# Order by hand to the last jump, a later token pass, and the last rows behind the jump, in attention with experts on one core

## The chip, the cores and the metric

The program runs on one core of a Trainium2 chip. A core has a matrix engine (TensorE, PE in the profile), a vector engine (VectorE, DVE), a scalar engine (ScalarE, ACT), GpSimd (POOL) and SyncE (SP), which only issues transfers. Each has an instruction queue of its own and works through it in order; they meet in semaphores. 16 DMA engines, shared by all queues, move data between HBM and the core's memory. The metric is the device time in microseconds (us); smaller is better.

## The reference

Block-sparse attention, then a layer of experts, in float32:

```python
# attention: 4 batches, 8 heads, 768 positions, 64 per head, blocks of 32
scores = scale * np.matmul(q, k.transpose(0, 1, 3, 2))
scores = np.where(mask, scores, -1e9)          # window, first and last block, 3 random blocks per row
attn = softmax(scores); x = attn @ v           # -> (3072 tokens, 512)
# experts: 8 of them, each token goes to its best one
expert_idx = np.argmax(x @ w_gate, axis=1)
gate_w = probs[arange(N), expert_idx]          # softmax of the logits
y = relu(x @ w1[e]) @ w2[e]                    # for the tokens of expert e: 512 -> 1024 -> 512
out = gate_w[:, None] * y
```

Which tokens go to which expert is known only at run time.

## The kernel before, in words

**Attention** takes the first 370 us or so. It is not touched, but for that its last part overlaps with the start of the experts.

**Tiles of the experts.** The tokens are sorted by expert into tiles of up to 128, of which every token has the same expert. `NS` = 21 tiles are always computed. The first `KA` = 5 are made of the tokens of the first three batches. What does not fill a tile goes to two *units* (up to 192 tokens, next to tiles 10 and 13, `AT`) and three *small tiles* (up to 32 tokens, next to tiles 10, 13 and 17, `AT_S`). Each tile, unit and small tile needs its own expert's weights, 2 MB for w1 and 2 MB for w2.

**One tile** i: `gather(i)` (L729, GpSimd) brings the token rows by an indirect transfer; `turn_x(i)` (L778) transposes them, on VectorE in blocks of 32 for later tiles; `layer1(i)` (L797, 64 matmul records, PSUM tile `hp` in two halves, then a relu into `hT` at L804); `layer2(i)` (L811, 16 records, PSUM tile `zp`; `weigh` at L816 multiplies with the gate weight into `zo`, and `put` at L826 scatters the rows by an indirect transfer on GpSimd). A small tile has `layer1_s` (`hps`, L865), `turn_h` (a transpose on PE, `tps_`, L874, slipped between the two halves of the next tile's layer 1) and `layer2_s` (`zps`, L882). A unit has `gather_u`, `turn_u` (24 transposes on VectorE, L904) and `layers_u`, which stand with a tile's layer 2 in a three-way jump on the unit's width.

**Weights.** SP issues all weight loads, in the order of the program: L758 for w1, L761 for w2. w1 and w2 have two buffers each, used in turns in the order of `orders`, which holds tiles, units and small tiles. So the load of position p + 2 waits until PE is done with position p: `fetch_after(what, layer)` asks for it behind the work that frees the buffer.

**The loop** `for i in range(NS)` puts, for each i: the gather of tile i + 3; a small tile's first layer; layer 1 of tile i + 1 with, between its halves, the transposes of tile i + 2; the small tile's second layer; gathers and transposes for coming units and small tiles; and layer 2 of tile i. At i = 2 follow two pieces that concern the rare cases and the small tiles. `judge()` (L383 to L392) counts on PE (`okp`, L386) whether all sums lie in a good range and writes `bad` and `arm` on VectorE, by which the last jump chooses between nothing more to do, some more tiles, and all of the work again in a safer way. `tokens_s()` (L704 to L711) spreads the small tiles' token numbers with a matmul (`tps`, L704) whose PSUM buffer is the one of `okp` (tag `xr`, one buffer), and makes from it the indices `gS` and `sS`.

**What sets the order.** Under `by_hand`, a manual schedule for GpSimd, PE and VectorE, the instructions of these three engines stand as the code puts them. It is closed at i = `KA` + 1 = 6. From there on a scheduler decides by its own costs, and so it may put later work ahead: for example `turn_u`, which the code has at i = 8, stands on VectorE right behind the work of `judge`, ahead of `bad`. Behind the loop is the last jump (L1064), and behind that the program's end.

Of the kernel before, what the change touches and what calls it, by code (L numbers as in the profile page):

```python
# [7 lines left out]
F32 = mybir.dt.float32  # L8
# [9 lines left out]
def kernel(  # L18
# [11 lines left out]
    nc = tc.nc  # L30
    P = 128
# [7 lines left out]
    N, DM = out.shape  # L39
# [332 lines left out]
    def judge():  # L372


        okp = ps_x.tile([1, 1], F32, name="okp", tag="xr")
        shape, total = [[4 * B * NPR, CW], [P, NT * E]], 0
        flats = (sums[:], lgn.rearrange("p t e -> p (t e)"))
        for j, (lo, hi) in enumerate(((2.0**-4, 2.0**40), (-(2.0**100), 2.0**100))):
            p, n = shape[j]
            total += p * n  # L380
            ok = mpool.tile([p, n], F32, name=f"ok{j}")
            okn = mpool.tile([p, 1], F32, name=f"okn{j}")
            nc.vector.tensor_single_scalar(ok[:], flats[j], lo, op=ALU.is_ge)  # L383
            nc.vector.scalar_tensor_tensor(ok[:], in0=flats[j], scalar=hi, in1=ok[:], op0=ALU.is_le, op1=ALU.mult)
            nc.vector.reduce_sum(okn[:], ok[:], axis=AX)
            nc.tensor.matmul(okp[:], lhsT=okn[:], rhs=ones[:p, :1], start=(j == 0), stop=(j == 1))  # L386
        bad = mpool.tile([1, 1], F32, name="bad")
        nc.vector.tensor_scalar(bad[:], okp[:], scalar1=float(total), scalar2=float(REDO), op0=ALU.not_equal, op1=ALU.mult)

        nc.vector.tensor_scalar_min(rt["more"][:], rt["more"][:], float(NC - NS))  # L390
        arm = rt["arm"] = mpool.tile([1, 1], I32, name="arm")
        nc.vector.tensor_max(arm[:], rt["more"][:], bad[:])  # L392
# [308 lines left out]
    def tokens_s():  # L701

        tp = ps_x.tile([P, KS], F32, name="tps", tag="xr")
        nc.tensor.matmul(tp[:], lhsT=rt["fourfold"][:], rhs=rt["tv"][:, NTB + 2 * KU :], start=True, stop=True)  # L704
        tv = sm.tile([P, KS], F32, name="tvS")
        nc.vector.tensor_copy(tv[:], tp[:])
        nc.vector.tensor_scalar(kept("gS", [P, KS])[:], tv[:], scalar1=0.0, scalar2=float(N - 1), op0=ALU.max, op1=ALU.min)
        none = sm.tile([P, KS], F32, name="noneS")
        nc.vector.tensor_scalar(none[:], tv[:], scalar1=0.0, scalar2=float(8 * N), op0=ALU.is_lt, op1=ALU.mult)
        nc.vector.scalar_tensor_tensor(tv[:], in0=tv[:], scalar=4.0, in1=none[:], op0=ALU.mult, op1=ALU.add)  # L710
        nc.vector.tensor_scalar(kept("sS", [P, KS])[:], tv[:], scalar1=rt["quarter"][:], scalar2=None, op0=ALU.add)  # L711
# [106 lines left out]
    def layer2(i, group):  # L818
        zp = upper["ps_z"].tile([P, DM], F32, name="zp")
        layer2_pe(i, zp)  # L820
        zo = xp.tile([P, DM], F32, name="zo")
        weigh(i, zo, zp)
        put(of("s", i, P), zo[:], group)
# [64 lines left out]
    def leave_s(k_, group):  # L888
        put(rt["sS"][:, k_ : k_ + 1], zo_s, group, out_s)
# [103 lines left out]
    for i in range(NS):  # L993
        if i == 0:
            ranks("B", TA, NT)
        gather(i + 3)
        here = AT_S.index(i) if i in AT_S else None
        if here is not None:
            layer1_s(here)
            fetch_after(("small", here), 1)  # L1000
        if i + 1 < NS:
            layer1(i + 1, lambda: turn_x(i + 2), *([turn_h] if here is not None else []))
            if i + 3 <= NS:
                fetch_after(i + 1, 1)
        if here is not None:
            layer2_s(here)
            fetch_after(("small", here), 2)
            leave_s(here, "rows_out")
        if i == 0:
            count("B")  # L1010
            layout_b()
        if i + 3 in AT:
            gather_u(AT.index(i + 3))
        if i + 3 in AT_S:
            gather_s(AT_S.index(i + 3))
        if i + 2 in AT:
            turn_u()
        if i + 2 in AT_S:
            turn_s()
        if i in AT:  # L1020

            continue
        if i + 1 in AT:


            u = AT.index(i + 1)
            zps = [upper["ps_z"].tile([P, DM], F32, name="zp") for _ in range(2)]
            zos = [xp.tile([P, DM], F32, name="zo") for _ in range(2)]
            banks = [upper["ps_h"].tile([P, DM], F32, name="hpu", tag="hp") for _ in range(2)]
            banks += [upper["ps_m"].tile([P, DM], F32, name="tpu", tag="tpg") for _ in range(2)] + zps[1:]  # L1030
            layer2_pe(i, zps[0])
            fetch_after(i, 2)
            for more in tc.Switch(index[u], 3):
                weigh(i, zos[0], zps[0])
                layers_u(u, P + more * QR // 2, banks)
                layer2_pe(i + 1, banks[1])
                weigh(i + 1, zos[1], banks[1])
            fetch_after(("unit", u), 1)
            fetch_after(("unit", u), 2)
            fetch_after(i + 1, 2)  # L1040
            put(of("s", i, P), zos[0][:], "rows_out")
            leave_u(u, "rows_out")
            put(of("s", i + 1, P), zos[1][:], "rows_out")
            continue
        layer2(i, "rows_out")
        if i + 2 <= NS:
            fetch_after(i, 2)
        if i == 1:
            tokens("B", NT, NB_)
        if i == 2:  # L1050
            judge()
            tokens_s()
        if i == 3:
            for u in range(KU):
                at = rt["xeU"][0:1, KU + u : KU + u + 1]
                index[u] = {
                    mybir.EngineType.PE: nc.tensor.value_load(at, min_val=0, max_val=2),
                    mybir.EngineType.Activation: nc.scalar.value_load(at, min_val=0, max_val=2),
                }
        if i == KA + 1:  # L1060
            by_hand.close()
    lent.close()

    for arm in tc.Switch(nc.values_load(rt["arm"][0:1, 0:1], min_val=0, max_val=REDO), REDO + 1):  # L1064
        inside = ExitStack()
        if arm < REDO:
            lend(inside, ps_h=2, ps_m=2, ps_z=2)
            last = NS + arm
            if arm > 1:
                for layer in (1, 2):  # L1070
                    fetch(NS + 1, layer)
            for i in range(NS, last):
                if i + 3 < last:
                    gather(i + 3)
                layer1(i, *([lambda: turn_x(i + 1)] if i + 1 < last else []))
                if i + 2 < last:
                    fetch_after(i, 1)
                layer2(i, "rows_out")
                if i + 2 < last:
                    fetch_after(i, 2)  # L1080
        else:
            lend(inside, ps_s=2, ps_t=1)
            attention_again()
            lend(inside, ps_h=2, ps_m=2, ps_z=2)
            ranks("A", 0, TA)
            count("A")
            layout_a()
            slots_a()
            for part in range(2):
                one_hots("A", rt["slA"], TA, KA, part)  # L1090
            tokens("A", TA, KA)
            ranks("B", TA, NT)
            count("B")
            layout_b()
            tokens("B", NT, NB_)
            tokens_s()
            for i in range(NC):
                gather(i)
                fetch(i, 1)
                fetch(i, 2)  # L1100
                turn_x(i)
                layer1(i)
                layer2(i, "rows_again")
            for j in range(KU):
                gather_u(j)
                for layer in (1, 2):
                    fetch(("unit", j), layer)
                turn_u()
                layers_u(j, MW, [upper["ps_h"].tile([P, DM], F32, name="hpu", tag="hp") for _ in range(2)] + [upper["ps_m"].tile([P, DM], F32, name="tpu", tag="tpg") for _ in range(2)] + [upper["ps_z"].tile([P, DM], F32, name="zpu", tag="zp")])
                leave_u(j, "rows_again")  # L1110
            for j in range(KS):
                gather_s(j)
                for layer in (1, 2):
                    fetch(("small", j), layer)
                turn_s()
                layer1_s(j)
                turn_h()
                layer2_s(j)
                leave_s(j, "rows_again")
        inside.close()  # L1120


# [28 lines left out]
```

## Time and profile before

| | us |
|---|---|
| time, median of 3 (lowest to highest) | 737.55 (736.49 to 738.51) |
| profiled run, span of the core | 735.2 |
| mean granted PE clock | 0.989 |
| PE busy | 708.9 |
| attention, layer 1 and layer 2 of the tiles on PE: s L233, hp L797, zp L811 | 159.5, 156.7, 134.0 |
| weight loads, 2 MB each | 54 |
| end of the last matmul, in the span | 720.05 |

A row of the profile's groups names line, engine, operation, and the tiles it writes and reads, then its count, its busy time, the mean of one in ns, and the idle time just ahead of it with what ended that. A row of the waits reads: which engine's line waited for which engine's line, us in all, times, longest. In a timeline, start and length come first; square brackets hold the idle time before, and its cause. In a table of stretches the busy times of the engines follow in the order PE, weight load, VectorE, ScalarE, GpSimd, then the granted clock, the DMA engines' share and GB/s. The digits of the slices are tenths.

### The profile page before, as it was taken

What the parts mean: (1) busy time and instruction counts of PE and PEld (TensorE: products, weight loads), DVE (VectorE), ACT (ScalarE), POOL (GpSimd) and SP (SyncE); (2) the same over time, 40 slices, a digit from 0 to 9 for tenths busy, and PEclk for the clock granted to TensorE, in tenths of its full rate; (3) what the DMA queues carried; (4) which work ended last, traced back from release to release, by engine and by line L of the source; (5) the groups of instructions that cost most, each with busy time, mean ns of one, the idle gap of its engine ahead of it and who ended that gap; (6) DMA issues with size and microseconds to landing.
All of it is one profiled execution on the core that took longest, in us unless ns stands there. A gap on an engine that the chain in (4) does not pass through costs nothing.

```text
span 735.2 us, 13091 instructions
## 1 busy us (share of the span) xinstructions
PE 708.9 (96%) x5142; PEld 455.2 (62%) x5142; DVE 398.8 (54%) x833; ACT 281.3 (38%) x454; POOL 72.4 (10%) x116
## 2 busy tenths in 40 slices
PE   7999999999999999999999899999999999999991
PEld 4555555555555555555777676776967786866750
DVE  4587778778678778999567434323124502332300
ACT  3667666766766675675411110111121121111110
POOL 6000000000000000000212111211132012111120
PEclk9999999999999999999999999999999999999996
DMA  8313323322332331292389879999779989999973
GB/s 195 76 34 86 87 65 90 86 60 50 87 88 66 87 87 48 63 396 64 83 296 330 326 267 356 309 347 348 268 286 401 376 306 363 371 395 368 391 278 112
DMA packets 117838, 154.33 MB, mean 210 GB/s; under 512 B 56307, under 2 KB 72755, under 8 KB 117748
## 3 DMA queue, kind: packets, MB, share of 16 engines
q1 hardware_dynamic: 111104, 138.23, 56.4%
q0 software_dynamic: 4512, 14.55, 5.2%
q8 instruction: 50, 0.82, 0.5%
q10 hardware_dynamic: 2132, 0.41, 0.3%
q14 instruction: 40, 0.33, 0.2%
HBM read 140.39 MB, written 12.88 MB: 208 GB/s over the span
## 4 chain that ended last, share of the span: by engine, by line
PE 81%; issue 12%; DVE 2%; POOL 2%; DMA 1%; ACT 0%; POOLq 0%
PE s L233 17%; PE op L254 17%; PE hp L797 14%; PE zp L811 10%; PE s L236 4%; PE sp L267 3%; PE xr L287 3%; PE tp L216 2%; PE hpu L811 2%; PE hpu L915 1%; PE hpu L923 1%; PE tpu L923 1%; PE tpu L915 1%; DMA ea<-x_rows,gB 1%; DVE ea L904 1%
## 5 line engine op out<-in xcount | busy, mean ns | idle before, releaser
L233 PE MATMUL s<-qT,kT 64*128 64x384 f32 x768 | 159.5, 494 | 0.9 <-ACT qT L218 0.9
L797 PEld LDWEIGHTS hp<-xgT,w 128*128 128x128 f32 x1344 | 154.7, 194 | 8.8 <-issue 6.8
L797 PE MATMUL hp<-xgT,w 128*128 128x128 f32 x1344 | 156.7, 277 | 0.9 <-ACT hT L804 0.9
L238 ACT ACTIVATE ea<-s 128x768 f32<-128x768 f32 x192 | 152.4, 812 | 7.3 <-PE s L236 5.5
L778 DVE STREAM_TRANSPOSE xgT<-xg 32x128 f32<-32x128 f32 x256 | 77.5, 303 | 128.9 <-PE hp L797 62.1
L811 PE MATMUL zp<-w,hT 128*128 128x512 f32 x304 | 134.0, 593 | 0.7 <-DMA w<-in_moe_w_dram 0.7
L244 DVE TENSOR_TENSOR esum<-esum,ea 128x768 f32<-128x768 f32 x128 | 122.6, 958 | 14.7 <-ACT ea L238 1.3
L254 PE MATMUL op<-ea,v_sb 128*64 128x384 f32 x768 | 129.3, 486 | 0.0
L254 PEld LDWEIGHTS op<-ea,v_sb 128*64 128x64 f32 x768 | 55.1, 137 | 68.8 <-issue 68.8
L811 PEld LDWEIGHTS zp<-w,hT 128*128 128x128 f32 x304 | 56.3, 190 | 65.5 <-issue 65.3
L233 PEld LDWEIGHTS s<-qT,kT 64*128 64x128 f32 x768 | 67.2, 190 | 38.4 <-issue 33.6
L274 DVE RECIPROCAL r<-ss 128x128 f32<-128x128 f32 x96 | 82.2, 912 | 1.3 <-ACT ss L269 1.3
L804 ACT ACTIVATE hT<-hp 128x512 f32<-128x512 f32 x40 | 23.9, 597 | 127.7 <-PE hp L797 115.8
L244 DVE TENSOR_TENSOR esum<-ea 128x768 f32<-128x768 f32 x32 | 30.6, 957 | 63.1 <-ACT ea L238 63.1
L236 PE MATMUL s<-pen,oh 64*128 64x384 bf16 x384 | 63.2, 326 | 0.0
L816 ACT ACTIVATE zo<-zp,xg 128x512 f32<-128x512 f32 x19 | 13.1, 687 | 125.4 <-PE zp L811 118.3
L259 ACT COPY oT<-op 128x384 f32<-128x384 f32 x32 | 15.3, 479 | 106.3 <-PE op L254 106.3
L236 PEld LDWEIGHTS <-oh 64*128 64x128 bf16 x384 | 18.9, 95 | 26.0 <-issue 1.2
L904 DVE STREAM_TRANSPOSE ea<-ea 32x128 f32<-32x128 f32 x48 | 13.8, 296 | 35.9 <-DMA ea<-x_rows,gB 35.3
L826 POOL DMA_INDIRECT out_dram<-zo,sB x16 | 16.1, 1008 | 171.3 <-ACT zo L816 136.4
L287 PEld LDWEIGHTS xr<-mix,oT 128*64 128x64 f32 (+1 forms) x372 | 24.0, 139 | 10.7 <-issue 10.7
L729 POOL DMA_INDIRECT xg<-x_rows,gA x5 | 6.1, 1226 | 220.6 <-ACT ea L238 219.4
(275 smaller groups left out, 450.9 us busy)
## 6 DMA issues: line engine op xcount, KB each, us to landing
w<-in_moe_w_dram SPq DMA_DIRECT2D x54, 2048.0 KB
k_sb<-in_k_dram SPq DMA_DIRECT2D x32, 192.0 KB
v_sb<-in_v_dram SPq DMA_DIRECT2D x16, 384.0 KB
x_rows<-xb SPq DMA_DIRECT2D x16, 384.0 KB
q_sb<-in_q_dram SPq DMA_DIRECT2D x30, 192.0 KB
sums<-ss SPq DMA_DIRECT2D x32, 3.0 KB
q_sb<-in_q_dram ACTq DMA_DIRECT2D x2, 192.0 KB
xg<-x_rows,gB POOLq DMA_INDIRECT x19, 7.7
```

Source lines behind the costliest of these rows:

```text
L233: nc.tensor.matmul(s[:, hh, :CW], lhsT=kT[r, c * P : (c + 1) * P], rhs=qT[r, cols], start=True, stop=False)
L236: nc.tensor.matmul(s[:, hh, :CW], lhsT=oh[r, c, :], rhs=pen[r, cols], start=False, stop=True)
L238: nc.scalar.activation(e, s[:, :, :CW], AF.Exp, scale=scale)
L244: nc.vector.tensor_add(t[:], es[(n, half, 0)] if c == 1 else t[:], e)
L254: nc.tensor.matmul(op[hh * D : (hh + 1) * D, :], lhsT=v_sb[:, hh, c, :], rhs=e[:, hh, :], start=(c == 0), stop=(c == NCH - 1),)
L267: nc.tensor.matmul(sp[hh * D : (hh + 1) * D, :], lhsT=ones[:], rhs=esum[:, hh, :], start=True, stop=True)
L274: nc.vector.reciprocal(r[:, m * P : (m + 1) * P], ss[:, m * P : (m + 1) * P])
L287: nc.tensor.matmul(xr[j * M_ : (j + 1) * M_, m, :], lhsT=oT[:, m * P + j * M_ : m * P + (j + 1) * M_], rhs=mix[:, pr, :], start=True, stop ...
L778: nc.vector.transpose(xT[d, :, t], xg[t, :DM].rearrange("p (c q) -> p c q", c=DB)[:, :, d])
L797: nc.tensor.matmul(hp[:, m, :], lhsT=st[i]["w1"][:, c, fb * P : (fb + 1) * P], rhs=st[i]["xT"][:, c, :], start=(c == 0), stop=(c == DB - 1),)
L804: nc.scalar.activation(hT[:, g * (FB // 2) : (g + 1) * (FB // 2), :], hp[:], AF.Relu)
L811: nc.tensor.matmul(zp[:], lhsT=st[i]["hT"][:, fb, :], rhs=st[i]["w2"][:, fb, :], start=(fb == 0), stop=(fb == FB - 1),)
```

## The change

Three edits. First, the hand order holds for the whole loop, up to the last jump. Second, the small tiles' token pass comes two tiles later, at i = 4, away from `judge`; `judge` stays at i = 2. Third, the last tile's result goes into a part of the unit's result buffer (`zo_u`), and its rows are put out behind the last jump, so that the jump does not come after that transfer in the order of GpSimd. In the rare case that does all of the work again, the indices are set to values outside the output, so that this late transfer writes nothing.

```diff
-        layer2(i, "rows_out")
+        if i + 1 < NS:
+            layer2(i, "rows_out")
+        else:
+
+            zp = upper["ps_z"].tile([P, DM], F32, name="zp")
+            layer2_pe(i, zp)
+            weigh(i, zo_u[:, 0, :], zp)
         if i + 2 <= NS:
             fetch_after(i, 2)
         if i == 1:
             tokens("B", NT, NB_)
         if i == 2:
             judge()
+        if i == 4:
             tokens_s()
...
-        if i == KA + 1:
-            by_hand.close()
+    by_hand.close()
     lent.close()
 
     for arm in tc.Switch(nc.values_load(rt["arm"][0:1, 0:1], min_val=0, max_val=REDO), REDO + 1):
...
                 leave_s(j, "rows_again")
+
+            nc.vector.memset(rt["sB"][:], 2 * N)
         inside.close()
+    put(of("s", NS - 1, P), zo_u[:, 0, :], "rows_out")
```

In the code's order, small tile 0 is followed by layer 1 of tile 12 and then layer 2 of tile 11 (i = 11), since tile 10 has its layer 2 inside the unit's jump and the loop goes on to the next i. The same holds for small tile 1 with tiles 15 and 14.

## The prediction

> **What bounds the kernel now.** I read the page first: is one engine full, and where is it not?
>
> ```profile
> PE 708.9 (96%) x5142; PEld 455.2 (62%) x5142; DVE 398.8 (54%) x833; ACT 281.3 (38%) x454; POOL 72.4 (10%) x116
> ...
> PE   7999999999999999999999899999999999999991
> ...
> PEclk9999999999999999999999999999999999999996
> DMA  8313323322332331292389879999779989999973
> ```
>
> TensorE (PE) is 96% busy, so time can come or go only where it stands still or its clock falls. The DMA row says more: from slice 22 on (the expert layers) the 16 DMA engines are nearly full too. A change of order there can turn a transfer in time into one that PE waits for. Next, all waits of PE:
>
> ```profile
> PE tps L704 <- DVE bad L388: 3.1, 1, 3.1
> ...
> PE tps__6201 L874 <- ACT ea L869: 0.9, 1, 0.9
> PE hp L797 <- ACT hT L804: 0.9, 2, 0.5
> PE zp L811 <- DMA w<-in_moe_w_dram: 0.7, 1, 0.7
> PE zps L882 <- ACT ea L875: 0.5, 1, 0.5
> ```
>
> This is what a better order can win in the expert layers: about 6 us, half of it in the token pass. Its stretch in the timeline:
>
> ```profile
> 411.36 0.30 PE L386 MATMUL okp<-ones,okn 64*1 64x1 f32 x4
> 414.76 0.38 PE L704 MATMUL tps<-tvB,fourfold 128*128 128x3 f32 x2 [3.10 <-DVE bad L388]
> 415.01 5.45 PE L797 MATMUL hp<-xgT,w 128*128 128x128 f32 x32
> ```
>
> The token matmul shares a PSUM buffer with `okp`, so it waits until VectorE has read `okp` into `bad`; VectorE was in the unit's 24 transposes (L904) until 414.5. The 32 matmuls behind it take 5.45 us, where the same 32 take 3.84 elsewhere: the granted clock fell to 0.5 for 3.41 us. So this place costs 3.1 + 1.6 = 4.7 us.
>
> Last, the stretch behind the first small tile, where the order will differ, PE and then the weight loads:
>
> ```profile
> 544.08 1.93 PE L865 MATMUL hps<-w,ea 128*32 128x256 f32 x32
> 545.94 3.84 PE L797 MATMUL hp<-xgT,w 128*128 128x128 f32 x32
> ...
> 554.24 1.96 PE L882 MATMUL zps<-w,ea 128*32 128x128 f32 x64
> 556.12 7.13 PE L811 MATMUL zp<-w,hT 128*128 128x512 f32 x16
> ```
>
> ```profile
> 544.18 0.37 SPq L761 DMA_DIRECT2D w<-in_moe_w_dram  x1
> 546.58 8.13 SPq L758 DMA_DIRECT2D w<-in_moe_w_dram  x2
> ```
>
> The loads at 544.18 and 546.58 are w2 of tile 11 and w1 of tile 12 (the group of two also holds w1 of 13, issued 554.34). Their landing events in the trace: w2 of the small tile 548.12, w2 of 11 555.88, w1 of 12 561.03, w1 of 13 566.88. A 2 MB w1 alone lands 8.1 us after issue; here it took 14.45, as it lands 5.1 us after the load ahead of it. A small tile needs 4 MB of weights like any other but gives PE only 1.95 + 1.9 us of work, so the loads fall behind there.
>
> **What the Trainium skill says.** "DMA: Bandwidth & Descriptors", "Queues, rings and completion order": each DMA engine takes a ring's descriptors in ring order. The landings above, in order of issue and 5 to 7 us apart, agree; so an early need of PE does not make a late load come sooner. "TensorE: Matmul & The Clock Gate", "HAM oscillation": an idle gap of about 3.4 us halves the clock[...]. The trace shows 3.10 us of idling, 3.41 us at 0.5 and 1.6 us lost: it agrees, with a slightly shorter gap. "Runtime: NRT & Kernel Launch", "Instruction fetch mechanics": a taken branch to code that isn't held must fetch it; at the last jump GpSimd stands 2.7 us behind its branch. "Perfetto Trace Analysis", "DMA Instruction — SWDGE (GPSIMD)": an indirect transfer's row ends with its descriptors, not with its data; the last put is 1.00 us long and lands 3.99 us after its start.
>
> **Part 1: the token pass two tiles later.** `tokens_s` now runs after layer 2 of tile 4, when `bad` is long written, and nobody needs its result before the first small gather, over 40 us on. The 3.1 us wait goes, and the cold clock with it: -4.7. The bad/arm operations also come ahead of the 24 transposes. These wait for later gathers now, but still lie 10 us or more ahead of the unit's first matmul, beside tiles that keep PE busy: 0.
>
> **Part 2: the hand order up to the end.** Comparing the instruction lists of both kernels engine by engine, the order of SP's weight loads is the same in both. PE's changes at three places.
>
> (a) Third small tile. Its transpose slips between the halves of layer 1 of tile 18, as in the first two. The waits of 0.95 and 0.46 go, a 0.47 wait like the one at the first two comes; the 0.72 us before the last `zp` goes, since its w2 is asked for sooner against its use. -2.1 + 0.5 = -1.7 (rounded up from -1.66).
>
> (b) First and second small tile. Before: `zps`, layer 2 of 11, layer 1 of 12 and 13. After: `zps`, layer 1 of 12, layer 2 of 11, layer 1 of 13. So PE wants w1 of 12 at the end of `zps`, 556.2, instead of at 563.1. It lands at 561.0: a new wait of 4.8 us, where the old order had 2.1 to spare. Can the load come sooner? It is issued when `hps` frees its buffer, just as before, behind the same two loads. If the queue were spaced as loads elsewhere (5.15 per w1, 6.3 per w2, 10.4 from issue when alone) it would be there 3.5 us after `zps`. One unit gather (two transfers at 541 to 542) moves out of this stretch, which helps a little: I take 4.3, range 3.5 to 4.9. For the second small tile the trace has the end of `zps` at 622.1 and w1 of 15 landed at 626.06: 4.0, by the even spacing 3.5; I take 3.9. Behind the waiting matmul stand layer 2 of 11 (or 14), whose weights are there, and everything after it. PE's queue is in order, so nothing of this is hidden; nor is it won back, as PE was solid to the end.
>
> (c) Third small tile again: layer 2 of 18 now comes before, not in the middle of, layer 1 of 20, 4 us sooner. Its w2 landed at 692.54 in the trace with PE there at 695.20, and the buffer that it loads into is freed by the same `zps`: 0 to 2 us of wait, I take 1.2. The second half of layer 1 of 18, or its first, may wait some tenths for its w1 (0 to 1): 0.2.
>
> Sum of new waits: 4.3 + 3.9 + 1.2 + 0.2 = +9.6.
>
> (d) Clock. If 3.1 us of idling sufficed once, about 4 should twice. Each costs at most the 1.6 measured; less when the half-speed stretch begins in the idle time. Range 0 to 3.2, I take 2.9.
>
> **Part 3: the last rows behind the jump.** Let T be the end of the last `zp`, 720.05 before. Before: ScalarE's weighing to T+0.8, put at T+1.05, landing T+5.0; GpSimd's end-of-loop wait for all its transfers ends there; 1.4 us semaphore work, the branch, 2.7 us fetch, a drain of 4.97 us from 729.43 to 734.40, end at T+15.2. After: that wait ends when put and gather of the tile before have landed, T+2.7 (722.79 in the trace), so 2.3 us sooner. Then the same 1.4 and 2.7, then the put, 0.7 + 1.0 us, and the drain. The put's landing, 3.99 from its start at about T+7.6, lies beside the drain. -2.3 + 1.7 = -0.6. If GpSimd's wait still covers something as late as the old put: +1.7; if the weighing's semaphore costs more, +2; if the branch work all lies beside the last matmul: -4.
>
> **Sum.** -4.7 - 1.7 + 9.6 + 2.9 - 0.6 = +5.5: 737.55 + 5.5 = 743.0 us.
>
> **Rivals.** *Clock holds.* The waits come, but the clock stays up: 743.0 - 2.9 = 740.1; with the waits at their low ends (7.0 in place of 9.6) 737.5. For: the gate looks at windows that run freely. Against: the 3.1 us gap did trip it.
>
> *Loads in time (the faster side).* No new wait: 737.55 - 4.7 - 1.7 - 0.6 = 730.5. For: alone such a load takes 8.1 us, and w1 of 12 is issued 9.6 us before PE wants it. Against: the queue ahead of it is unchanged, the DMA row shows nines there, and the busy share from 557 to 584 us is full:
>
> ```profile
> 557.00:584.00 27.00, 27.00 (x159) 19.80 (x157) 13.52 (x45) 3.08 (x5) 3.89 (x4) 1.00 1.01 384
> ```
>
> *More waits.* Waits at their upper ends (4.9 + 4.2 + 2 + 1 = 12.1), clock 3.2 and a tail of +2: -4.7 - 1.7 + 12.1 + 3.2 + 2 = +10.9, 748.4. For: each wait of PE delays the free of a buffer and with it later loads. Against: those loads have 5 to 12 us in hand.
>
> **How the numbers follow.** Forecast 0.60, clock holds 0.20, loads in time 0.12, more waits 0.08. The bounds of 0.3% are 735.3 and 739.8. Faster: the third case and a little of the second's low end with a cheap tail, 0.14. Same: the second case below 739.8 and the low end of the first, 0.17. Slower: 0.69. The range from 736.5 to 747.5 leaves out the loads in time and most of the last case: under 2 in 10.
>
> **What would show it.** In the changed profile: no wait at L704, and the 32 matmuls behind the judge back at 3.84; the chain and PE's waits headed by L797 waiting for `w<-in_moe_w_dram`, twice about 4 us, right after each of the first two `zps`, followed by `hp` groups longer than their 3.84 per 32; from T to the end about 14.5 us. No such waits at L797 would overthrow (b), and with it the sign. A wait at `zp` L811 of more than 2 us would mean that I mis-sized (c).

## The result, and the profile after

The changed kernel takes 746.91 us (median of 4, 744.98 to 748.07) against 737.08 us (median of 4) for the kernel before: the ratio is 1.0128, with a 95% interval of 1.0099 to 1.0156. It is slower by 9.8 us; the forecast was 5.5. A later set of runs gave 745.17 against 736.16, ratio 1.0134 (1.0104 to 1.0163).

The page first, slices and engines:

```profile
PE 710.3 (96%) x5142; PEld 456.8 (61%) x5142; DVE 397.7 (54%) x833; ACT 281.2 (38%) x454; POOL 72.0 (10%) x116
...
PE   7999999999999999999999999999979997999891
PEld 4555555555555555555876677677767767766560
...
PEclk9999999999999999999999999999999999999997
DMA  8313333331233232391499999999599979999963
```

In the PE row, the two sevens in slices 30 and 34 are new. They stand where the first two small tiles are. In these two slices the DMA row is at nine; in the slice just ahead of each it is at five and at seven. Now all waits of PE (line waited, line waited for, sum, times, longest):

```profile
PE hp L797 <- DMA w<-in_moe_w_dram: 9.0, 3, 4.4
...
PE zp L811 <- DMA w<-in_moe_w_dram: 2.5, 1, 2.5
...
PE hp L797 <- ACT hT L804: 0.9, 2, 0.5
```

The waits at L704, L874 and L882 are gone, as they should be; in their place PE waits for weights, 11.5 us in all. PE's timeline at the judge, then at the first, second and third small tile:

```profile
411.21 0.31 PE L386 MATMUL okp<-ones,okn 64*1 64x1 f32 x4
411.44 3.84 PE L797 MATMUL hp<-xgT,w 128*128 128x128 f32 x32
```

```profile
549.40 1.96 PE L882 MATMUL zps<-w,ea 128*32 128x128 f32 x64
555.10 9.01 PE L797 MATMUL hp<-xgT,w 128*128 128x128 f32 x64 [3.75 <-DMA w<-in_moe_w_dram]
```

```profile
610.33 2.52 PE L865 MATMUL hps<-w,ea 128*32 128x256 f32 x32
...
621.07 1.95 PE L882 MATMUL zps<-w,ea 128*32 128x128 f32 x64
627.40 8.71 PE L797 MATMUL hp<-xgT,w 128*128 128x128 f32 x64 [4.38 <-DMA w<-in_moe_w_dram]
```

```profile
673.74 3.81 PE L797 MATMUL hp<-xgT,w 128*128 128x128 f32 x32 [0.87 <-DMA w<-in_moe_w_dram]
...
690.13 7.31 PE L797 MATMUL hp<-xgT,w 128*128 128x128 f32 x64
699.90 7.13 PE L811 MATMUL zp<-w,hT 128*128 128x512 f32 x16 [2.46 <-DMA w<-in_moe_w_dram]
```

Behind the judge there is no wait left and the 32 matmuls take 3.84 us. Behind each of the first two `zps` PE stands still about 4 us, and the 64 matmuls then take 9.01 and 8.71 us; the same 64 take 7.31 us at 690.13. By the landing events w2 of 11 is there at 549.85 and w1 of 12 at 554.96, 5.1 us behind it: PE starts layer 1 of 12 at 555.10. Layer 2 of 11, whose weights were there long before, stands behind it in PE's order and starts at 563.95. The table of stretches shows the clock there (PEclk is the number ahead of the DMA share), with one stretch behind the third small tile to compare:

```profile
549.00:566.00 17.00, 13.25 (x138) 11.79 (x137) 8.92 (x33) 2.16 (x4) 4.84 (x5) 0.90 1.03 402
610.00:640.00 30.00, 25.16 (x237) 20.67 (x237) 8.35 (x28) 4.09 (x8) 4.93 (x5) 0.94 1.01 377
664.00:708.00 44.00, 40.67 (x287) 27.44 (x286) 14.53 (x48) 6.06 (x11) 5.00 (x5) 1.00 1.00 379
```

Clock 0.90 over 17 us is 3.4 us at half speed; 0.94 over 30 us is 3.6. The sum, by the two profiles (from the start of `okp` to the last `zp`, then the tail):

| step | forecast | in the profile |
|---|---|---|
| token pass: wait and half-speed stretch gone | -4.7 | -4.8 |
| third small tile and last `zp`: waits gone | -1.7 | -2.1 |
| new waits for weights: tile 12, 15, 18 layer 1, 18 layer 2 | 4.3 + 3.9 + 0.2 + 1.2 = 9.6 | 3.75 + 4.38 + 0.87 + 2.46 = 11.5 |
| half-speed stretches | 2.9 | 1.7 + 1.4 = 3.1 |
| second small tile's first layer, 2.52 for 2.27 | none | 0.3 |
| last `zp` to the end | -0.6 | 15.3 for 15.15: 0.1 |
| sum | 5.5 | 8.1 (spans 743.2 and 735.2: 8.0) |

The profiled run was the quickest of its four; the median adds 1.9 us (0.8 us in the later set) that no profile of this kernel shows.

### The profile page after: what moved, and what is told of

The parts are those of the page before. It is cut to its first block, busy times and chain, and to the rows that moved or that the text cites. A ratio compares the mean times of both kernels' runs of the same rounds, so it can differ in the third digit from the quotient of the medians.

```text
span 743.2 us, 13102 instructions
## 1 busy us (share of the span) xinstructions
PE 710.3 (96%) x5142; PEld 456.8 (61%) x5142; DVE 397.7 (54%) x833; ACT 281.2 (38%) x454; POOL 72.0 (10%) x116
## 4 chain that ended last, share of the span: by engine, by line
PE 80%; issue 12%; DMA 3%; POOL 1%; DVE 1%; ACT 0%; POOLq 0%
PE s L233 17%; PE op L254 17%; PE hp L797 14%; PE zp L811 11%; PE s L236 4%; PE sp L267 3%; PE xr L287 3%; PE tp L216 2%; PE hpu L811 2%; DMA w<-in_moe_w_dram 2%; DMA out_dram<-zo,sB 1%; PE tpu L923 1%; PE hpu L923 1%; PE hpu L915 1%; PE tpu L915 1%
## 5 line engine op out<-in xcount | busy, mean ns | idle before, releaser
L797 PE MATMUL hp<-xgT,w 128*128 128x128 f32 x1344 | 158.7, 279 | 9.9 <-DMA w<-in_moe_w_dram 9.0
L259 ACT COPY oT<-op 128x384 f32<-128x384 f32 x32 | 15.3, 478 | 106.0 <-PE op L254 106.0
L267 PE MATMUL sp<-esum,ones 128*64 128x384 f32 x128 | 27.7, 512 | 0.0
L287 PE MATMUL xr<-mix,oT 128*64 128x136 f32 (+1 forms) x372 | 27.7, 279 | 0.0
```

Source lines behind the costliest of these rows:

```text
L267: nc.tensor.matmul(sp[hh * D : (hh + 1) * D, :], lhsT=ones[:], rhs=esum[:, hh, :], start=True, stop=True)
L287: nc.tensor.matmul(xr[j * M_ : (j + 1) * M_, m, :], lhsT=oT[:, m * P + j * M_ : m * P + (j + 1) * M_], rhs=mix[:, pr, :], start=True, stop ...
L797: nc.tensor.matmul(hp[:, m, :], lhsT=st[i]["w1"][:, c, fb * P : (fb + 1) * P], rhs=st[i]["xT"][:, c, :], start=(c == 0), stop=(c == DB - 1),)
```

## The experiments

**Only the token pass** (built on the kernel before):

```diff
         if i == 2:
             judge()
+        if i == 4:
             tokens_s()
```

> Only the token pass is moved, from tile 2 to tile 4; order by hand still ends at tile 6, and the last put stands before the jump. My step (part 1): the 3.1 us wait at L704 goes and with it the half-speed stretch, 4.7 us in all, so about 732.5 us (ratio about 0.994). Rival: the time comes back later as waits for weights, since the loads are issued when PE frees their buffers and the DMA engines are nearly full: then 735 to 737.

Measured: 733.17 us against 736.44, ratio 0.9962 (0.9949 to 0.9975), so 1.8 to 3.8 us less. The direction is that of part 1, the size is smaller than 4.7. The timeline shows both:

```profile
410.39 0.30 PE L386 MATMUL okp<-ones,okn 64*1 64x1 f32 x4
410.63 3.84 PE L797 MATMUL hp<-xgT,w 128*128 128x128 f32 x32
```

```profile
PE hp L797 <- issue: 1.4, 1, 1.4
...
PE tps__6201 L874 <- ACT ea L869: 0.5, 1, 0.5
...
PE zp L811 <- DMA w<-in_moe_w_dram: 0.3, 1, 0.3
```

The wait and the slow matmuls are gone in full, and they did not turn into waits for weights (0.3 us, 0.7 before), which was the rival. One standstill of 1.4 us at a layer 1 is new, with no releaser in the profile. From `okp` to the last put this profile is 4.05 us shorter (410.39 to 716.08, against 411.36 to 721.10), which is the 4.7 and 0.8 of smaller waits less that standstill. What the standstill is was not settled, nor why the times differ by less still.

**Only the order by hand up to the jump:**

```diff
-        if i == KA + 1:
-            by_hand.close()
+    by_hand.close()
```

> Only the order by hand reaches to the last jump; token pass at tile 2 and last put as before. Theory: this edit alone carries the whole loss. Layer 1 of tile 12 (15) comes ahead of layer 2 of 11 (14) and waits about 4 us for its w1 each time, with a half-speed stretch behind each. The wait at L704 goes in this kernel too, since the unit's transposes no longer stand ahead of bad on VectorE; some tenths of a wait for bad stay. So 746 to 748 us, as the changed kernel. Rival 1: without moving the token pass the 3.1 us and the cold clock stay, so 751 to 752. Rival 2: the loss is in the late put: then about 737 or faster.

Measured: 745.99 us against 736.44, ratio 1.0153 (1.0132 to 1.0174): this edit alone carries the whole loss.

```profile
PE hp L797 <- DMA w<-in_moe_w_dram: 10.5, 3, 4.8
...
PE zp L811 <- DMA w<-in_moe_w_dram: 2.1, 1, 2.1
...
PE tps L704 <- DVE more_f L390: 0.2, 1, 0.2
```

The last line is of interest: with the token pass still right behind the judge, the wait at L704 is 0.2 us, not 3.1. The 24 transposes no longer stand ahead of `bad`. So in the changed kernel the later token pass brings some tenths at most; the hand order alone had already removed that wait. Rival 1 (the 3.1 us stay) falls, and so does rival 2 (the loss is in the late put). The waits behind the first two small tiles are longer here than in the changed kernel's profile:

```profile
555.68 9.57 PE L797 MATMUL hp<-xgT,w 128*128 128x128 f32 x64 [4.81 <-DMA w<-in_moe_w_dram]
...
628.25 9.01 PE L797 MATMUL hp<-xgT,w 128*128 128x128 f32 x64 [4.67 <-DMA w<-in_moe_w_dram]
```

By the clock records of the trace, the half-speed stretch at the first of them is 6.83 us long; at the second, and at both places in the changed kernel, it is 3.41 us.

**Only the last put behind the jump:**

```diff
-        layer2(i, "rows_out")
+        if i + 1 < NS:
+            layer2(i, "rows_out")
+        else:
...
+            weigh(i, zo_u[:, 0, :], zp)
...
+    put(of("s", NS - 1, P), zo_u[:, 0, :], "rows_out")
```

> Only the last tile's put goes behind the jump. My forecast for this part was 0.6 us less, between 4 less and 2 more. The tail of the changed kernel's profile is 15.3 us from the last matmul to the end against 15.2, so now I expect no change: 737 us within 1. A rival that puts the unexplained 4 us of the result here expects 740 to 741.

Measured: 736.93 us against 736.44, ratio 1.0000 (0.9991 to 1.0009). No change within 0.7 us, so the unexplained 4 us are not here; but 0.6 us, the forecast for this part, would not show in these times either. The profile of this run:

```profile
414.06 6.68 PE L797 MATMUL hp<-xgT,w 128*128 128x128 f32 x32
...
713.88 7.11 PE L811 MATMUL zp<-w,hT 128*128 128x512 f32 x16 [2.04 <-SPq L1070]
...
728.59 1.00 POOL L826 DMA_INDIRECT out_dram<-ea,sB  x1 [13.40 <-issue]
```

Here the put starts 7.6 us after the last matmul, as worked out, and from that matmul to the end it is 14.4 us, 0.8 less than before. The span is the same because two things went the other way: the half-speed stretch behind the judge is 6.83 us long where it was 3.41, so that the 32 matmuls take 6.68 us in place of 5.45, and PE waits 2.04 us ahead of the last `zp`, not 0.72. (The profile names SP; w2 of the last tile lands at 713.75, 0.13 us before that `zp`.) Whether the put has a part in either is not shown. The put in the changed kernel:

```profile
727.95 0.69 ACT L816 ACTIVATE ea<-zp,xg 128x512 f32<-128x512 f32 x1 [6.13 <-PE zp L811]
736.42 1.00 POOL L826 DMA_INDIRECT out_dram<-ea,sB  x1 [12.03 <-issue]
```

It starts 8.5 us after the last matmul. With the put behind the jump, GpSimd's wait at the end of the loop ends when the loop's last gather has landed: 2.0 us after the last matmul in the put-only run (722.99), 3.2 us in the changed kernel (731.15). In the kernel before, that gather landed 2.74 us after the last matmul. In the changed kernel the last two `zp` follow each other without a wait, so the last matmul comes sooner after that gather's start. A wait saved ahead of the last `zp` is thus in part given back in the tail.

**SP's loads in the order in which PE now wants them** (built on the changed kernel; w1 of 12 ahead of w2 of 11, w1 of 15 ahead of w2 of 14):

```diff
             fetch_after(("small", here), 1)
+            if i in AT:
+                fetch_after(i, 2)
...
-            fetch_after(i + 1, 2)          # behind the unit's jump
```

> The changed kernel with one more edit: SP issues w1 of tile 12 ahead of w2 of tile 11 (and 15 ahead of 14), the order in which PE now wants them. Same matmul order, same bytes. Theory (it is the place in the queue that makes the load late): w1 of 12 lands about 8 us after the small tile's first layer, before the small tile is done; both waits of about 4 us and the half-speed stretches go (3.75 + 1.7 + 4.4 + 1.4 = 11.2), so 735 to 736 us, faster than the kernel before. Rival (the DMA engines are too full, whatever the order): the wait only moves to w2 of 11 (14) at L811, some 4 us each again, and the time stays at 744 to 747.

Measured: 733.13 us against 736.44, ratio 0.9960 (0.9945 to 0.9975). The loads, and PE behind the first small tile:

```profile
540.38 0.37 SPq L758 DMA_DIRECT2D w<-in_moe_w_dram  x1
540.96 0.82 SPq L761 DMA_DIRECT2D w<-in_moe_w_dram  x1
```

```profile
548.54 1.95 PE L882 MATMUL zps<-w,ea 128*32 128x128 f32 x64
550.42 7.41 PE L797 MATMUL hp<-xgT,w 128*128 128x128 f32 x64
557.67 7.03 PE L811 MATMUL zp<-w,hT 128*128 128x512 f32 x16
```

By the landing events w1 of 12 is there at 549.00, 8.6 us after its issue (13.25 us in the changed kernel), and w2 of 11 at 556.24, ahead of its use at 557.67. The same bytes and the same matmuls; only the place of two pairs of loads in the queue differs. That settles it against a mere lack of DMA bandwidth at this place.

**Layer 2 of 11 (14) first, as the kernel before had it** (built on the changed kernel):

```diff
+        early = i - 1 in AT
+        if early:
+            layer2(i, "rows_out")          # ahead of layer 1 of tile i + 1, not behind it
         if i + 1 < NS:
             layer1(i + 1, ...
```

> The changed kernel with one more edit: behind the first and second small tile, PE takes layer 2 of tile 11 (14) ahead of layer 1 of tile 12 (15), as the kernel before did; the loads keep their order. Theory (PE asks for w1 before it can be there): the waits at L797 behind the first two small tiles and their half-speed stretches go, 11.2 us, so 735 to 736 us; since the order of the loads gave 733 by the other way round, 733 is possible too. Rival (order by hand costs something else, on VectorE or GpSimd, that the load order happened to hide): 740 or more.

Measured: 733.12 us against 736.16, ratio 0.9953 (0.9938 to 0.9967). The only wait for weights that is left is 1.7 us at layer 1 of 18:

```profile
PE hp L797 <- DMA w<-in_moe_w_dram: 1.7, 1, 1.7
```

So either side can be turned: the loads to suit the matmuls, or the matmuls to suit the loads. The gain is some 2 us more than I expected; why is not settled. The 2.46 us wait at layer 2 of 18 has gone too.

**The waits filled with matmuls of no use** (built on the changed kernel; nothing of the result is left out):

```diff
+        if i - 1 in AT:
+            idle = upper["ps_m"].tile([P, P], F32, name="idle2", tag="tpg")
+            for _ in range(14 if i == 11 else 17):
+                nc.tensor.matmul(idle[:], lhsT=ident[:], rhs=ident[:], start=True, stop=True)
         if i + 1 < NS:
             layer1(i + 1, ...
```

> The changed kernel, with matmuls of no use put on PE ahead of layer 1 of tile 12 (14 of them, about 3.4 us) and of tile 15 (17, about 4.1 us), in the time in which PE waits. The waits for w1 stay as long in sum, only filled. Theory (the idle gap makes the clock fall): the half-speed stretches behind go, 1.7 + 1.4 us, and the time is some 3 us below the changed kernel, 743 to 744. Rival (the longer layer 1 behind the wait is slow weights or something else, not the gap): no change, 746 to 747, or more if the matmuls come on top.

Measured: 743.01 us against 736.16, ratio 1.0080 (1.0056 to 1.0104); the changed kernel beside it 745.17.

```profile
550.97 3.39 PE L1004 MATMUL idle<-ident 128*128 128x128 f32 x28
555.11 7.38 PE L797 MATMUL hp<-xgT,w 128*128 128x128 f32 x64 [0.75 <-DMA w<-in_moe_w_dram]
```

```profile
620.75 4.06 PE L1004 MATMUL idle<-ident 128*128 128x128 f32 x34
625.62 7.38 PE L797 MATMUL hp<-xgT,w 128*128 128x128 f32 x64 [0.80 <-DMA w<-in_moe_w_dram]
```

Layer 1 behind the wait is back at 7.38 us, 1.6 and 1.3 less than in the changed kernel, though its weights came no sooner: it was the idle gap that cost the clock. A part is given back as waiting. Fill and rest make 4.1 and 4.9 us in place of 3.75 and 4.38. The wait at layer 2 of 18 grows, and brings a half-speed stretch of its own (the same 16 matmuls take 7.13 us in the changed kernel):

```profile
PE zp L811 <- DMA w<-in_moe_w_dram: 3.1, 1, 3.1
...
696.53 8.83 PE L811 MATMUL zp<-w,hT 128*128 128x512 f32 x16 [3.12 <-DMA w<-in_moe_w_dram]
```

**Loads at the third small tile too** (built on the load order run; w2 of 18 ahead of w1 of 20):

```diff
-            if i + 3 <= NS:
+            if i + 3 <= NS and i != 17:
                 fetch_after(i + 1, 1)
...
             fetch_after(("small", here), 2)
+            if i == 17:
+                fetch_after(i + 1, 1)
```

> The kernel of the run load_order, and behind the third small tile SP also issues w2 of tile 18 ahead of w1 of tile 20. Theory (again the place in the queue): the 0.8 us wait for w2 of 18 goes, w1 of 20 lands 6 us later with 6 us in hand: about 0.8 us less than load_order, 732.3. Rival: the DMA engines are full by now, and the wait moves on to w1 of 20 or w2 of 19: no change, 733.

Measured: 731.87 us against 736.16, ratio 0.9948 (0.9930 to 0.9965). It beats both kernels, but its interval overlaps that of the load order run, so the step from that one isn't shown by the times. The profile shows the 0.8 us wait at `zp` gone, and 2.2 us in place of 1.8 at layer 1 of 18:

```profile
PE hp L797 <- DMA w<-in_moe_w_dram: 2.2, 1, 2.2
```

**The changed kernel again:**

> The changed kernel once more, unedited, beside the others on the same chip. Its profile counted 744.98 us, the fastest of its four runs, and the others had a mean clock of 0.977 to 0.979 where that had 0.988. If the half-speed stretches behind the waits vary in length from run to run, a second profile shows the same waits within some tenths and another sum of slow matmuls; if the waits themselves vary, it shows waits that differ by 1 us or more. Expected 745 to 748.

Measured: 745.17 us (744.36 to 747.8). The second profile:

```profile
554.50 8.89 PE L797 MATMUL hp<-xgT,w 128*128 128x128 f32 x64 [3.91 <-DMA w<-in_moe_w_dram]
...
626.37 8.80 PE L797 MATMUL hp<-xgT,w 128*128 128x128 f32 x64 [3.90 <-DMA w<-in_moe_w_dram]
```

The waits differ by 0.2 and 0.5 us from the first profile, the slow layer 1 by 0.1. That is too little for runs 3 us apart, and this profile too is of the quickest run. The mean clock doesn't sort the runs either (747.8 us at 0.984, 745.85 at 0.988; in the first set 748.07 at 0.984, 746.15 at 0.977). The hand-order run shows that waits and half-speed stretches at the first two small tiles can come out longer, by 1.1 and 0.3 us of waiting and by 0.6 and 0.3 us of slow matmuls against the first profile. Whether that makes the unprofiled runs up to 3 us longer is not shown.

## Why the prediction was right, step by step

The sign and the mechanism were right, and the time lay within the range. The size was too small: 9.8 us for 5.5, with 746.9 us close to the range's upper end. The waits for weights come to 11.5 us, nearer to the 12.1 of *More waits*, to which I gave 0.08, than to the 9.6 of the forecast.

- **Part 1, the token pass**: the 3.1 us and the half-speed stretch went. The reason given was only half of it: by the hand-order run, bringing `bad` ahead of the transposes does nearly all of it (0.2 us left), and moving `tokens_s` alone does so too (token-pass run).
- **Part 2 (a)**: 2.1 for 1.7. The 0.47 wait that I added does not come.
- **Part 2 (b)**, which carried the forecast: 3.75 and 4.38 us (3.91 and 3.90 in the second profile) for 4.3 and 3.9. That the sum comes so close (8.1 for 8.2) is in part luck: the first was 0.55 too high and the second 0.48 too low. The two runs that turn the order of loads or of matmuls show the cause: w1 stands behind a w2 that isn't needed yet.
- **Part 2 (c)** was mis-sized: 0.87 + 2.46 for 0.2 + 1.2, and 2.46 lies beyond the 2 that I gave as its upper end. I said that a wait of over 2 us at `zp` would mean this. I took the landing of the kernel before over as it was. But `zps`, which frees the buffer of w2 of 18, comes behind the first layer of tile 18 in the new order, so that PE wants this w2 14.1 us after its issue (683.29, wanted at 697.4) where it had 17.2 us before (677.96 to 695.20); and it took 16.56 us to land, 14.58 before.
- **Part 2 (d)**: 3.1 for 2.9, and the filled waits show it to be the gap.
- **Part 3**: 0.1 for -0.6 in the profile of the changed kernel, where the put starts 8.5 us after the last matmul, 0.9 later than worked out. I took the landing of the loop's last gather from the kernel before (2.74 us after the last matmul), though part 2 moves the last matmul against it: it became 3.2, which is 0.5 of the 0.9. Alone the edit gave a tail 0.8 shorter, and a time that is the same within 0.7 us.
- **Not foreseen**: the 0.3 us in the second small tile's first layer, and the 0.8 to 1.9 us between profiled run and median.
- **Readings that were off, without weight in the sum**: the landings around w1 of 12 lie 5.2 to 7.8 us apart, not 5 to 7. The w1 that took 8.1 us (issued at 570.43) had a load ahead of it; one with nothing ahead took 7.9 (527.14). For the second small tile the even spacing gives 3.2, not 3.5.

## What to carry to other kernels

With transfers in a queue like this one, where loads land in the order of their issue and the DMA engines are nearly full, the order of the loads and the order of their uses must be written as one. If one is turned and the other isn't, the engine waits for a load that stands behind one not yet needed, and here that cost more than the small waits that the new order removed. Look at such a place in the trace by landing times: a load that lands late and long after its issue need not be slow, it may be behind something (13.25 us after its issue here, 8.6 with the two loads turned). And when several edits go together, run each alone: here one edit lost 9.5 us in sum, and hid that it had also won most of the 4.7. The token pass alone, an edit of one line, takes 733.17 us, as little as the whole change with its loads or its matmuls turned (733.13 and 733.12).

## What the runs showed of the hardware

- The half-speed stretch comes behind idle gaps of 3.07 us and more (put-only run; 3.1 in the kernel before, and again at `zp` in the filled run, where the clock was 0.96 over the 44 us from 664, that is 3.5 us at half speed), but not behind gaps of 2.46 us (changed kernel, 1.00 over the same stretch) and 2.65 us (its second profile).
- In the clock records of every trace, all changes of the clock lie a multiple of 3.413 us apart, wherever the gaps are: in the changed kernel the two stretches begin at 555.11 and 626.79, which is 21 times 3.413, the first as the wait ends and the second 0.6 us before its wait ends. The stretches behind a gap are 3.41 or 6.83 us long, and gaps of one length can cost differently: 3.10 us of idling brought 3.41 us at half speed in the kernel before, 3.07 us brought 6.83 in the put-only run. Only the part that falls on work costs time, half of itself: 1.7 us at 555.11, 1.4 at 626.79.
- "HAM oscillation" in the Trainium skill's "TensorE: Matmul & The Clock Gate" warns of gaps over about 3.4 us; here 3.07 us sufficed. It counts 1.67 us at half speed behind each gap, half of that lost; the stretches here are 3.41 or 6.83 us long and cost 1.4 to 2.8 us.
- The last put lands 2.76 us after its start behind the jump, where no weight load is under way (the last landed at 731.63), and 3.99 us ahead of it, where one is until 723.78.
